# A fused threshold attention and gated MLP on one core: its 4602 steps in another order, and its PSUM banks handed out anew

## The chip, the core and the metric

The kernel runs on one core of a Trainium2 chip. The metric is device microseconds of one execution, from the first to the last instruction of that core with what lies around them. Its engines are TensorE (PE, with its weight loads as PEld), VectorE (DVE), ScalarE (ACT), GpSimd (POOL) and SyncE (SP), which here only issues transfers. Each runs its own list of instructions in order and waits for the others by semaphores. PSUM, where PE writes its results, has 8 banks.

## The reference

Attention with a threshold, over 8 batches and 8 heads (576 positions, 64 wide), feeds a gated MLP (512 in, 1024 inner, half of it a gate that mixes positions):

```python
scores = scale * np.matmul(q, k.transpose(0, 1, 3, 2))
thresh = np.max(scores, axis=-1, keepdims=True) - tau
scores = np.where(scores >= thresh, scores, -1000000000.0)
attn = np.exp(scores - np.max(scores, axis=-1, keepdims=True))
attn = attn / (np.sum(attn, axis=-1, keepdims=True) + 1e-09)
x = np.matmul(attn, v)                       # heads side by side: (8, 576, 512)
h = gelu_tanh(x @ w_in)
u, v = h[..., :512], h[..., 512:]
v_n = (v - mean(v)) / sqrt(var(v) + 1e-06) * g_ln
v_s = np.einsum('ts,bsd->btd', w_sg, v_n) + b_sg[None, :, None]
return x + (u * v_s) @ w_out
```

## The kernel before

Two heads are one attention, so there are 32 (n = 0 to 31), four to a batch, and behind each batch its MLP. The function doesn't compute where it is called: each step (a piece of work on one engine, or a transfer) goes into a list, `plan`, of 4602 steps. At the end `issue` runs through them in the order of a table of numbers, ORDER, that `table` unpacks; where an exponential follows a gelu or the other way round, it adds an ACT table load and a small activation on a spare column (L1156). The order in which the steps are issued is the order in which each engine's list stands. A second table, FIRST_BANKS, gives each PSUM tile its bank in the order of the steps; a step that writes a bank waits until the last reader of what lay there is done. So one table sets what stands behind what on every engine, the other who waits for whom at the banks.

The steps of an attention with n of 4 and more, with the names that the rows have:

- scores (L547): for a tile of 128 rows of one head, four matmuls of 288 columns (`ks`, `klz` with `qst`), six for the tile of both heads' last rows (`kl` with `qtail`). Nine tiles.
- DVE takes the negated maxima of the rows (L556, `maxima_of`); POOL makes the threshold of it (L562, with `columns`); ACT the exponentials (L583, into `p_0` to `p_3`, or `pm` for the tile of last rows); DVE keeps those over the threshold and sums each row (L590, "select"), after which the scores' bank is free.
- DVE turns blocks of 32 by 32 of the exponentials (L605, and L601 for `pm`) into `turned`.
- PE multiplies these with the values `v` (L743): 18 blocks, each with 8 small matmuls on tiles of 32 rows by 64 columns, in six steps of 24 (a row "x72" in an order below is three such steps; each matmul is recorded twice in the trace, so 144 there). ACT takes the result from PSUM (L750).
- The inverses of the row sums go from DVE (L628, L654) through DRAM and back (L658, L662: two transfers of SP's queue), and POOL multiplies with them (L754, `ir`). ACT and POOL split the result into two parts, `xh` and `xl` (L771, L776).

The MLP of a batch is made of products (L841) with weights split in two parts: v (512 columns, `wih`, `wil` with `xh`, `xl`), u, the spatial gate (`wsh`, `wsl` with `z`), down (`woh`, `wol` with `gh`, `gl`). Around them are gelu on ACT (L830), the normalisation (L920 to L957 on DVE, POOL and ACT), the fold of the last 64 rows on DVE (L901, `vt`), and the gate (L995 DVE, L1011 ACT, L1015 POOL). The first four attentions take another way (L527, and transpositions on PE, L252). The MLP of a batch lies in time beside the attentions of the next one, woven by ORDER.

Of the kernel before, what the change touches and what calls it, by code (L numbers as in the profile page):

```python
# [22 lines left out]
P = 128  # L23
# [10 lines left out]
    "c-m!H2V4|K-`=^q-Mixsj*cL`_a+ewsHjP7!4hMOCN}J`BpTamd83IX(bx;95H%W&5le_I5mbm3r1#zg1n!P<{g`iOW)FRT-|vo{otghU&+{)cy9Y%<_Jb~{"  # L34
    "g#h21{<taAE$Ki=M*2*vaF<;P$sh-Z*O5tli)Y|FGIjuxWt?#z=qE8zQhl73J~C*6#eaR=IMD!zuJ^#u0Dv3`766C=S%fW+9UdnG+)~Ki6Eif1r^pbR>*G;I"
    "v=Sh3Y=c=5Mjs>==mQBfQN%jRL(9<@c?}2_M3^`#fLqUEVk!#0*CNlbJEjN_WUL$^^|9D2KE%WnClZ;V0nP<3awJi>i^ZXNf`LN-`z7>o;e?n3`$Tc^GE-sk"
    "l(-k54lxp|#43F4rSLsOw?GV4EQ**?QS2W(qK18DYA!Bf6+$&b78FE_5x5AVQ87d-&=(n*u{ThKphOU=MHHTd2v0<@6bKXdAWI0b84JmdL2QZHMU<Kn^-^XO"
    ")nld>vFp@am5A6I7NNhQkt%issv%a(4vN$wH4A~JSa!CH;jve05i5rs6k{gVkRn%=X-<s@L@F^w@X&}z&FvR7X{vN?1H7LhcA7(g5DP#9tR!|4UDzScfP$<y"
    "7>t#|aU!n?H)3PESOqJB4IWv7u4o;FC1EwFp$H*1fOsu3qtrMx$a!{@!qXH7fM`%OkvTgKDQ<vlNz8?okWT-`=eDRR2BzA?eL@I{7!n;KlOi4?OG3ilQbadS"
    "CBi}FfhD6WB(71Mt3(^bqD45BIAwS_u|W6S0{lhf7#?@AcNBIKM-CrrsD&ajKs+HtBnB*jMySD|!hyrSv3bIi??OXy=Vbp;O8B_*lj5onBU6x6E9ONF2`Mxs"  # L40
    "kE{`L`60--V`AY9G`Jx?_Ma<Uw?Bg<okB_j`<3AEYf!OKXqd!_03k~*oe+C1#Cd%8Ai%`zGVYOpBgtYxicla8LJd;J{^14@p%L7t$c#|Um5>nEG26j3LgXep"
    "i{r~SIPiEKvcqr?O&|-h<20E49Xw71>QK1Feh^C3gPagf7ev~SDN@c+i8OctdykwFB5?G@@nRbd{?kCy^9>_IOlLZk$s8s$1%e{M;3Q&ZO}`RE-fvA|VsxP>"
    "(wO=<nnH@$Ag?Kc!tFa#v?=Tn$pS@i`ya<#R!s4MCIKjp5a)n&HIU5WOj4wQ1f19qD?CL&An}aE9GP(CL-<Wv;Ct^PBrGUgLd4EaYfXtFtXvhDWN1Vt;bfY@"
    "*~e?S;E@VMz?3OskaL6L0)wN6Qm<wDD^c@)SSaG?yIkRQY{Q_9VhSS~(Biyt2fmQ(03l}r$pDTQ-Ybv`AE^&CL-r0=Qkan}#TCp@ra_I6@S+B-fm%X`bZ96>"
    "Yl^1Oqyz_>OAQ9+YJ}=PqWTYO2H7%L2Dad4F{c)#11};-DA?#+;LZ?Xzc<7Q?yBV?#Bf-wLQ0FR7*m-t$Op{DurXvkU~#qmqOg$=jj<WR)0l+O;(12Ppr}J6"
# [71 lines left out]
Q = 32  # L117
# [1046 lines left out]
```

## Time and profile before

| | us |
|---|---|
| timed runs, median of 3 | 861.12 |
| lowest, highest | 858.95, 861.51 |
| profiled execution | 867.9 |
| its span, first to last instruction | 866.0 |
| mean granted clock of TensorE in it | 0.988 |

| engine | busy us | share of the span |
|---|---|---|
| PE | 829.8 | 96% |
| DVE | 679.7 | 78% |
| ACT | 602.0 | 70% |
| POOL | 583.4 | 67% |

Busy time is counted where an engine runs an instruction; waiting for a semaphore is idle time. What ended an idle time stands behind it as a releaser; "issue" is idle time in which the engine waited for nothing that the profile shows. The granted clock is 1.00 at full speed; 0.50 is the lower of two levels.

### The profile page before, as it was taken

How to read it: one execution, taken by the hardware profiler on the slowest of the kernel's cores; microseconds unless marked ns; L12 is line 12 of the kernel's file. 1: busy time of each engine (PE TensorE's matmuls, PEld its weight loads, DVE VectorE, ACT ScalarE, POOL GpSimd, SP SyncE). 2: the span in 40 equal slices, each digit the busy share in tenths (PEclk: the TensorE clock that was granted, in tenths of full speed). 3: DMA queues.
4: the chain of work that ended last, by engine and by line, in shares of the span. 5: the costliest groups of instructions: out<-in, count | busy, mean ns of one | idle time of the engine just before them, and what ended most of it. 6: DMA issues, size and time to landing. Idle time of an engine off the chain costs nothing.

```text
span 866.0 us, 30568 instructions
## 1 busy us (share of the span) xinstructions
PE 829.8 (96%) x12590; PEld 743.3 (86%) x12590; DVE 679.7 (78%) x1288; ACT 602.0 (70%) x1093; POOL 583.4 (67%) x966
## 2 busy tenths in 40 slices
PE   7999999988999999899999999999999999899998
PEld 5566789987889988899889988999899998799998
DVE  7898978976699888778887899789897988777110
ACT  5899987554976678666797468866688647774243
POOL 4885576573776667565867487856778567655486
PEclk8999999998999999999999999999999999999999
DMA  6645146554456565456555575465646656433101
GB/s 211 229 123 149 32 126 173 162 164 129 122 155 183 172 177 172 112 170 171 154 153 161 155 200 166 124 176 172 183 130 178 177 157 166 119 104 86 39 8 62
DMA packets 80190, 125.57 MB, mean 145 GB/s; under 512 B 13746, under 2 KB 36274, under 8 KB 80051
## 3 DMA queue, kind: packets, MB, share of 16 engines
q1 hardware_dynamic: 80050, 123.62, 49.4%
q8 instruction: 99, 1.62, 0.8%
q14 instruction: 41, 0.33, 0.1%
HBM read 70.55 MB, written 9.90 MB: 93 GB/s over the span
## 4 chain that ended last, share of the span: by engine, by line
PE 43%; DVE 4%; ACT 4%; issue 3%; POOL 2%; DMA 2%; SPq 1%; POOLq 0%; DVEq 0%; ACTq 0%
PE all_banks L841 28%; PE all_banks L547 8%; PE all_banks L743 7%; DVE maxima_of L556 2%; ACT p L583 1%; DVE p L590 1%; DMA ir<-ld 1%; ACT L1156 1%; DVE turned L605 1%; POOL free L1048 1%; POOL ot L1048 1%; SPq L662 0%; DMA rq<-in_qT 0%; SPq L470 0%; DMA ks<-khi 0%
## 5 line engine op out<-in xcount | busy, mean ns | idle before, releaser
L583 ACT ACTIVATE p<-all_banks,maxima_of 128x576 f32<-128x576 f32 x256 | 182.7, 738 | 95.3 <-DVE maxima_of L556 90.8
L556 DVE TENSOR_REDUCE maxima_of<-all_banks 128x1 f32<-128x576 f32 x288 | 206.8, 742 | 40.4 <-PE all_banks L547 33.0
L590 DVE SCALAR_TENSOR_TENSOR p<-all_banks,maxima_of,p 128x576 f32<-128x576 f32 x256 | 201.3, 806 | 42.3 <-ACT p L583 24.7
L547 PE MATMUL all_banks<-ks,qst 128*128 128x288 f32 x560 | 155.2, 310 | 7.9 <-DVE p L590 4.3
L605 DVE STREAM_TRANSPOSE turned<-p 128x1152 f32<-128x1152 f32 x112 | 152.4, 1367 | 7.2 <-PE all_banks L743 6.2
L743 PE MATMUL all_banks<-turned,v 32*64 32x144 f32 x8064 | 147.3, 286 | 11.1 <-issue 10.7
L743 PEld LDWEIGHTS all_banks<-turned,v 32*64 32x64 f32 x8064 | 127.6, 130 | 25.4 <-issue 22.8
L562 POOL TENSOR_TENSOR maxima_of<-columns,maxima_of 128x1 f32<-128x1 f32 x288 | 53.2, 191 | 115.7 <-DVE maxima_of L556 110.9
L547 PE MATMUL all_banks<-klz,qst 128*128 128x288 f32 x448 | 125.5, 298 | 0.0
L547 PEld LDWEIGHTS all_banks<-ks,qst 128*128 128x128 f32 x560 | 102.9, 190 | 22.2 <-DVE p L590 11.8
L841 PE MATMUL all_banks<-wsh,z 128*128 128x288 f32 (+2 forms) x512 | 111.7, 299 | 3.1 <-DVE pm L590 2.0
L1156 ACT ACT_TABLE_LOAD x81 | 103.9, 1283 | 1.5
L841 PEld LDWEIGHTS all_banks<-wsh,z 128*128 128x128 f32 x512 | 85.1, 190 | 4.7 <-DVE pm L590 2.2
L547 PEld LDWEIGHTS all_banks<-klz,qst 128*128 128x128 f32 x448 | 85.5, 191 | 1.8 <-issue 1.2
L841 PE MATMUL all_banks<-gh,woh 128*128 128x288 f32 (+2 forms) x256 | 75.8, 300 | 0.5 <-ACT ot L1045 0.5
L841 PE MATMUL all_banks<-gh,wol 128*128 128x288 f32 (+2 forms) x256 | 75.1, 296 | 0.0
L841 PE MATMUL all_banks<-wsl,z 128*128 128x288 f32 (+2 forms) x256 | 75.0, 297 | 0.0
L841 PE MATMUL all_banks<-xl,wih 128*128 128x288 f32 (+2 forms) x256 | 74.5, 296 | 0.0
L841 PE MATMUL all_banks<-xh,wil 128*128 128x288 f32 (+2 forms) x256 | 74.4, 295 | 0.0
L841 PE MATMUL all_banks<-xh,wih 128*128 128x288 f32 (+2 forms) x256 | 74.0, 296 | 0.0
L841 PE MATMUL all_banks<-gl,woh 128*128 128x288 f32 (+1 forms) x240 | 70.9, 299 | 2.5 <-POOL gl L1015 2.2
L1048 POOL TENSOR_TENSOR ot<-ot,xl 128x288 f32<-128x288 f32 (+1 forms) x60 | 47.8, 800 | 23.7 <-ACT ot L1045 23.4
(150 smaller groups left out, 1890.8 us busy)
## 6 DMA issues: line engine op xcount, KB each, us to landing
v<-in_vR SPq DMA_DIRECT2D x112, 288.0 KB, 3.5
ks<-khi SPq DMA_DIRECT2D x112, 144.0 KB, 3.2
rq<-in_qT SPq DMA_DIRECT2D x28, 320.0 KB, 4.3
qst<-qhi SPq DMA_DIRECT2D x56, 160.0 KB, 3.3
qst<-rq SPq DMA_DIRECT2D x56, 160.0 KB, 2.8
rk<-in_kT SPq DMA_DIRECT2D x28, 288.0 KB, 4.4
klz<-kl SPq DMA_DIRECT2D x56, 144.0 KB, 2.6
ir<-ld SPq DMA_DIRECT2D x56, 144.0 KB, 3.9
```

Source lines behind the costliest of these rows:

```text
L547: nc.tensor.matmul(sc[:, a, 0:HALF], w, x, start=(j == 0), stop=(j == len(terms) - 1))
L556: nc.vector.tensor_reduce(nmax, st["s", h, i][:, :, 0:HALF], AX.XY, ALU.max, negate=True)
L562: nc.gpsimd.tensor_tensor(thr, toff, st["nm", h, i], ALU.subtract)
L583: nc.scalar.activation(target(h, i), st["s", h, i][:, :, 0:HALF], AF.Exp, bias=st["nm", h, i])
L590: nc.vector.scalar_tensor_tensor(dst, st["s", h, i][:, :, 0:HALF], st["thr", h, i], dst, ALU.is_ge, ALU.mult, accum_out=st["l"][:, c:c + 1])
L605: nc.vector.transpose(out, st["p", i].rearrange("p (h k x) -> p k h x", h=2, x=Q))
L743: nc.tensor.matmul(st["accs"][g // 2][hs, g % 2, 0:W], st["v"][rows, o:o + D], st["turned"][rows, k, h * W:(h + 1) * W], start=(k == 0), s ...
L841: nc.tensor.matmul(st["acc"], *term(j), start=(j == 0), stop=(j == n - 1))
L1048: return lambda: nc.gpsimd.tensor_tensor(o(), o(), x[b, m][:, ts_], ALU.add)
L1156: tables[kind]()
```

## The change

Only the two tables change: ORDER, with the same 4602 steps in another order, and FIRST_BANKS. The code below them is the same, two lines further up in the file, so L743 is L741 after, L547 is L545, L841 L839, L754 L752, L562 L560, L605 L603, L590 L588. All matmuls are the same ones, 12590 in the trace. As exponentials and gelus stand in another sequence, `issue` adds two more table loads (84 switches for 82).

```diff
 ORDER = (
-    "c-m!H2V4|K-`=^q-Mixsj*cL`_a+ewsHjP7!4hMOCN}J`BpTamd83IX(bx;95H%W&5le_I5mbm3r1#zg1n!P<{g`iOW)FRT-|vo{otghU&+{)cy9Y%<_Jb~{"
...
 FIRST_BANKS = (
-    "c-l3R3lak{2txgP{~PyVw$o{5V-SJFw%nq|tut!JDkj6NSj{8HBD(-YS~c5BimM%nspK4jar(?HWA%AFD`a)pc1;UnP79di&}i?nWhlpK!+cAjNA+UD6oU;i"
...
```

What it moves is seen in the engines' lists. First PE in the values of attention 29, from the first of them on (before; in the trace this begins at 742.08 us):

```order
L743 MATMUL all_banks<-turned_11212,v_29_11287 64x144 x72
L547 MATMUL all_banks<-ks_1_11260,qst_138 128x288
L547 MATMUL all_banks<-klz_141,qst_138 128x288
...
L743 MATMUL all_banks<-turned_11212,v_29_11287 64x144 x48
L547 MATMUL all_banks<-ks_1_11260,qst_138 128x288
L547 MATMUL all_banks<-klz_141,qst_138 128x288
L547 MATMUL all_banks<-ks_1_11260,qst_138 128x288
L547 MATMUL all_banks<-klz_141,qst_138 128x288
L743 MATMUL all_banks<-turned_11212,v_29_11287 64x144 x24
L841 MATMUL all_banks<-wih_110,xh_9597 128x512
```

and the same place after:

```order
L741 MATMUL all_banks<-turned_11210,v_29_11297 64x144 x48
L545 MATMUL all_banks<-ks_1_11299,qst_138 128x288
L545 MATMUL all_banks<-klz_141,qst_138 128x288
...
L741 MATMUL all_banks<-turned_11210,v_29_11297 64x144 x72
L545 MATMUL all_banks<-ks_1_11299,qst_138 128x288
L545 MATMUL all_banks<-klz_141,qst_138 128x288
L545 MATMUL all_banks<-ks_1_11299,qst_138 128x288
L545 MATMUL all_banks<-klz_141,qst_138 128x288
L839 MATMUL all_banks<-wih_110,xh_9596 128x512
L839 MATMUL all_banks<-wil_114,xh_9596 128x512
L839 MATMUL all_banks<-wih_111,xh_10067 128x512
L839 MATMUL all_banks<-wil_115,xh_10067 128x512
L741 MATMUL all_banks<-turned_11210,v_29_11297 64x144 x24
```

The values come in pieces of 48, 72 and 24 where they came in 72, 48 and 24, with ten matmuls of the scores between the first two in both, and the last piece now stands behind four wide products. As many matmuls of PE lie ahead of the first row in both orders.

Then POOL, at the multiplication with the inverses of attention 13 (355 to 362 us), before:

```order
L562 TENSOR_TENSOR maxima_of<-columns,maxima_of 128x1
L927 TENSOR_SCALAR bn_4_5142<-bn_4_5142 64x1
L931 TENSOR_TENSOR bn_4_5142<-bn_4_5142,columns 64x1
L935 TENSOR_SCALAR bn_4_5142<-bn_4_5142 64x1
L754 TENSOR_TENSOR ir_5039<-v_13_4808,ir_5039 128x576
L562 TENSOR_TENSOR maxima_of<-columns,maxima_of 128x1 x3
L942 TENSOR_TENSOR vv_4_5115<-vv_4_5115,g_bc 64x512
L440 TENSOR_TENSOR kl<-rk_4887,khi_5144 128x576
```

and after:

```order
L929 TENSOR_TENSOR bn_4_5151<-bn_4_5151,columns 64x1
L560 TENSOR_TENSOR maxima_of<-columns,maxima_of 128x1
L933 TENSOR_SCALAR bn_4_5151<-bn_4_5151 64x1
L438 TENSOR_TENSOR kl<-rk_4890,khi_5144 128x576
L560 TENSOR_TENSOR maxima_of<-columns,maxima_of 128x1 x2
L940 TENSOR_TENSOR vv_4_5116<-vv_4_5116,g_bc 64x512
L752 TENSOR_TENSOR ir_5040<-v_13_4776,ir_5040 128x576
L955 TENSOR_TENSOR zt_101<-vv_4_5116,zt_101 64x512
```

The multiplication stood ahead of three thresholds and now stands behind them.

Last DVE in the scores of attention 9 (237 to 244 us), before:

```order
L605 STREAM_TRANSPOSE turned_3221<-p_0_2994 128x18x2x32
L556 TENSOR_REDUCE maxima_of<-all_banks 128x1 x3
L590 SCALAR_TENSOR_TENSOR pm,sums_of<-all_banks,maxima_of,pm 128x576
L605 STREAM_TRANSPOSE turned_3221<-p_1_3112 128x18x2x32
L901 TENSOR_TENSOR vt_3281<-all_banks,vt_3281 64x512
L590 SCALAR_TENSOR_TENSOR p_2_3272,sums_of<-all_banks,maxima_of,p_2_3272 128x576
```

and after:

```order
L603 STREAM_TRANSPOSE turned_3226<-p_0_3005 128x18x2x32
L554 TENSOR_REDUCE maxima_of<-all_banks 128x1 x3
L603 STREAM_TRANSPOSE turned_3226<-p_1_3147 128x18x2x32
L588 SCALAR_TENSOR_TENSOR p_2_3267,sums_of<-all_banks,maxima_of,p_2_3267 128x576
L899 TENSOR_TENSOR vt_3279<-all_banks,vt_3279 64x512
L588 SCALAR_TENSOR_TENSOR p_2_3267,sums_of<-all_banks,maxima_of,p_2_3267 128x576
L588 SCALAR_TENSOR_TENSOR pm,sums_of<-all_banks,maxima_of,pm 128x576
```

The select of pm, which came ahead of the second turn, is now the last of these. On PE the four matmuls of the next scores now take the bank that the first select of p_2 frees; in before they took the bank of pm.

## Rows read from the trace of the kernel before

**Rows 1.** Page, busy time: the span, and busy us (share) xinstructions of each engine

```profile
span 866.0 us, 30568 instructions
...
PE 829.8 (96%) x12590; PEld 743.3 (86%) x12590; DVE 679.7 (78%) x1288; ACT 602.0 (70%) x1093; POOL 583.4 (67%) x966
```

**Rows 2.** Lines: op, names, shapes xcount, busy us, mean ns, idle us before <-releasers

```profile
L547 PE MATMUL all_banks<-ks,qst 128*128 128x288 f32 x560 | 155.2, 310 | 7.9 <-DVE p L590 4.3 <-issue 2.6 <-ACT v L750 0.3
L743 PE MATMUL all_banks<-turned,v 32*64 32x144 f32 x8064 | 147.3, 286 | 11.1 <-issue 10.7 <-DVE uu L995 0.3
```

**Rows 3.** PE's time line: start, us, operation xcount, [idle before <-releaser]

```profile
196.18 2.50 PE L743 MATMUL all_banks<-turned,v 32*64 32x144 f32 x144 [2.08 <-issue]
...
205.38 0.78 PE L743 MATMUL all_banks<-turned,v 32*64 32x144 f32 x14 [2.83 <-issue]
...
330.08 0.54 PE L547 MATMUL all_banks<-ks,qst 128*128 128x288 f32 x2 [1.59 <-issue]
```

**Rows 4.** Page, DMA queues: packets, MB, share of 16 engines

```profile
q8 instruction: 99, 1.62, 0.8%
```

**Rows 5.** Windows: us, then busy us (xcount) of PE, PEld, DVE, ACT, POOL, PEclk, DMA, GB/s

```profile
235.86:330.07 94.21, 90.25 (x1655) 82.23 (x1655) 84.72 (x156) 67.91 (x117) 66.39 (x108) 1.00 0.59 169
```

**Rows 6.** PE's time line, attention 29

```profile
742.08 2.51 PE L743 MATMUL all_banks<-turned,v 32*64 32x144 f32 x144
...
745.91 0.29 PE L547 MATMUL all_banks<-ks,qst 128*128 128x288 f32 x1 [0.65 <-issue]
...
747.05 1.78 PE L743 MATMUL all_banks<-turned,v 32*64 32x144 f32 x96
...
752.12 0.74 PE L743 MATMUL all_banks<-turned,v 32*64 32x144 f32 x28 [1.80 <-issue]
...
753.12 0.39 PE L841 MATMUL all_banks<-wil,xh 128*128 128x512 f32 x1
753.35 0.40 PE L841 MATMUL all_banks<-wih,xh 128*128 128x512 f32 x1
```

**Rows 7.** Windows, the stretches of lower granted clock (eighth column, PEclk)

```profile
200.00:220.00 20.00, 17.16 (x209) 14.82 (x208) 12.75 (x24) 10.95 (x18) 7.73 (x16) 0.83 0.46 129
320.00:340.00 20.00, 18.40 (x319) 16.84 (x306) 13.67 (x24) 15.90 (x28) 15.04 (x22) 0.91 0.53 149
360.00:380.00 20.00, 18.64 (x307) 18.12 (x311) 14.84 (x27) 11.60 (x21) 12.98 (x21) 0.91 0.52 150
```

**Rows 8.** PE's time line, three idle times put down to DVE and POOL

```profile
361.36 0.40 PE L841 MATMUL all_banks<-wsh,z 128*128 128x288 f32 x1 [1.97 <-DVE pm L590]
...
438.40 0.40 PE L547 MATMUL all_banks<-ks,qst 128*128 128x288 f32 x1 [1.35 <-DVE p L590]
...
610.41 0.40 PE L841 MATMUL all_banks<-gl,woh 128*128 128x288 f32 x1 [1.25 <-POOL gl L1015]
```

**Rows 9.** POOL's time line, attention 13

```profile
358.89 1.40 POOL L754 TENSOR_TENSOR ir<-v,ir 128x576 f32<-128x576 f32 x1 [2.59 <-ACT vv L939]
360.25 0.47 POOL L562 TENSOR_TENSOR maxima_of<-columns,maxima_of 128x1 f32<-128x1 f32 x3
```

**Rows 10.** DVE's time line, attention 9

```profile
236.99 1.38 DVE L605 STREAM_TRANSPOSE turned<-p 128x1152 f32<-128x1152 f32 x1 [0.79 <-PE all_banks L743]
238.30 2.05 DVE L556 TENSOR_REDUCE maxima_of<-all_banks 128x1 f32<-128x576 f32 x3
240.27 0.80 DVE L590 SCALAR_TENSOR_TENSOR pm<-all_banks,maxima_of,pm 128x576 f32<-128x576 f32 x1
...
242.29 0.64 DVE L901 TENSOR_TENSOR vt<-all_banks,vt 64x512 f32<-64x512 f32 x1
```

**Rows 11.** PE's time line, attention 9: the idle time in the same stretch

```profile
242.99 0.40 PE L841 MATMUL all_banks<-wsh,z 128*128 128x288 f32 x1 [0.59 <-DVE vt L901]
```

**Rows 12.** Page, the costliest groups: the table loads of ACT

```profile
L1156 ACT ACT_TABLE_LOAD x81 | 103.9, 1283 | 1.5
```

**Rows 13.** PE's time line, the start

```profile
13.52 0.69 PE L252 MATMUL all_banks<-ident_r,p 128*128 128x128 f32 x2 [2.14 <-DVE p L590]
```

More of the change, by code (lines that the diff above doesn't have):

```diff
@@ L38 @@
[L38 to L45, printed above, removed]
@@ L98 @@
[L98 to L100 removed]
+    "c-n1P30zcF)PLtOZ{7?u0}QC3?4Tfvptxq>hUS)Nrj=SQh?-k!i&k1$xm0SYNv^n?TDj$txuX~=iVGm1Ae#%a4lv9<bHBU10l)9}Ilk@QbN=Ul{`cJb?t|kv"
+    "gz$mS_=@l7Jv$+(i#ES<hnN}bc5nzB^iDdl9_iF_0qg}d1VT>VSNoiB5)lVbD@3sYw>mh9nq=*S2IOpP;lT1h4tRwLamOtVMw}v2H-}{Bzz7bolR&(k1E&U<"
@@ new lines @@
+    "2ku4=9<c`!0XGpp+(B?0G%?&tFdgh5PAn2>CnO0j(9pz$V2}=AoG6NvCN{v`gbO9e039St5|Mat&dezw<&9W7foP?SfMIY{O^LqqmP$wsrLjc>TMEiaS(0vt"
+    "B(SqAh$qdRQl}uu;Y#blfE$$t{GSdMI9xe{61x~kEG1{ap7hMoj%GT(&S6%PcBCMUN+XS<q*)r32B(jKQ*fM7K_L;oa*AeG8WnrsE@Ys13etdYh%K=sHq8<}"
+    "a#HG520PDj3M2WklA#e5%+1J($k~O@N~xrA9AqSBxB>SPVn*Vrz^zDWRN$QGk2qp%!V!ZhX?lb<BE3ioOQN;P${tbcM5BN$CM2eT01|a+IE>ty047164cG;d"
+    "c9I3<N$8T`l%s<2p}{#~hG-)TM?GowB%E|B%~IA#V@e14F%YZ->7lvOq%k+jKvI%4v_48b&iX~@e?PMp24rlJh9rtuh8$6qBQZGzb0ZO*D$?q}4Fro^NH;?z"
@@ new lines @@
+    "j)<mD`;9Ck!e07kWPw_+6p~cVIv{6h!6QyIDm4@(5pcW7nGI5~VKlNE7MAj(Wy&EV3*pp*7A+Z6&Z%$fLMtu6A`_ROaV={n2_%)1g2_(wW9hYw7WU*sHad*A"
+    "b6{J3m^kMwS!bFpwJFj8WfM;t1gTIIMv>-CVj`2%g-XKF+)W%UJ`S0Pp=feeyAxY9kv4odE1sxDftW2tGSNqBBy#vF8mX~}m?f<|d=X9Lz!o%R91_zsA(0Yc"
+    "Ff1B<pg81A(HUPHp0<)qh%2SYd|KB%7RM<J&6xJ%W<=Q$EQ~;IC~=HQvuE(ckEP<A>NI_ZN!ukUa0^An=oH#S!6iD3qbQ{$wsbHz$^<b7DND)=nOdz0M?!|O"
+    "Lo}E(U94)$0JP-FB#;J68aSFFiHaeJ80?Xq7&&rKEs#X6l`M&GVgpLb1KS}fK}mP!&(NIJ!kJp?g5^pXG2z5lVzrz(gctx*L8==ZQqqD(rYTc)92H$O<2E@b"
@@ new lines @@
+    "S+hhr=YUcUoRcbzKq`@=s<o(xCxqy1<D7LWN>Ny%xLa;!?Br$|iK9X|GowQ(XVDlEAtvd}G%!*5*j#0jJ7<ze8{}rWBoCb{5)-L}NH9V{5}Uxv8Im+il%{Bw"
+    "(*kdi{gvIE(~e~>Z6HN6_sXV@Dup;ne6fY8iHR&#xO44i<s(&_S(+bm`an`=?c^DmiDb^#hTM#pnsl}i(U4ivl=u@*IaPx#5x9@Thp9znM14iGh-1p>LLiNf"
+    "+$@qvaubbelBOp0mO^r722a_sGfvmcri&bzS)pQ3Gt-T5AW?7+BE!Qm7c8<_&axtR<bmi;`{^D{GGxiq_zaU6(dd*3O^nhaaY?I$Dkr|oiZYV3ZtBG`DqO2>"
+    "1X{4rjM$rzBG9BcDM`YeFr;Ha9Fdt}P${LmmTv`irS7dC6%5h&pAcgw%2&dmVQ4fu8dN{IS)xy(QvIDDEmTo6_sZ7=V$e)Fvjo91k%CYKne0vr8WG7YtSp#B"
@@ new lines @@
+    "EknhGk~nclpad98ITf7^1d_^*4U#h=$AS@TDKUn^wWjIBqJvMQmlBuinaxlODFZrAh-5Ff2=u~)VY-{8$wSJ+LM$wDR#c>V1Wu|JX$TOqFqYI=aHiNYMu?6z"
+    "$4NuNNeLh}U7X@L#bpzNl_}29f&}Wx-XM~UsP$VC$<5sV^TEkd!CXmlE!#uF4zUVGEwxK429KYBENs-V4=G=KA+RJjoS?v2h<+Bfp%=_8+Z&QFjgOs(A9f<%"
+    "IAaSjqmM*D+(|)512Lvc7D2`jBthC|p)@5X0)`L>3LP-w)RHG{C)nhkhNjZDC?!~&TOy98LBdjQ1ewIfA;^RC<C&$5&xkQZ)R5Yfpo~1Wk&r1-PSVIi+$iz?"
+    ")9TcRdeb`sNBt=n>5$?{xziAoBx6m%7>qO`l&;0843(V<&17T@sR>m|ut<>+6N?(qCaNnbTzW6nlZ3-e2{T5G`V&IV4K>MEvXZu8&TSWgK#Z8cbfHnGGeWPH"
@@ new lines @@
+    "Xv=fUBlpT59-O=L*1v8zSHo9ZT0iw#uhKV=^TU&CL2vywZ2jBHD{MHf_0Ke~PA~3%1#G3|{N3Qe(HkGPe?8yaeDl5D3nuXivp2%BM!8L}xao&qP$paz>IJ0`"
+    "na4+E@`)L7kmra>m-FtX_&fF}g+-^*d+Jh*m-wuxim+@MA6yVsp?CAHjMNpkF*d^7|BRLGgU)w_CxOqt*ru+q+6@k+%;4cb!q}|(mqu-HzZ2T>AXI_u!F=h2"
+    "!?rLRYUpv<A@g%@w&{lFIn;OjUE~F!R`-}QK60D9IB4)COWeJ%(qd&K^3I1u^#RMk6Wv`3M;s19<sChq)c35f6D{7Zjb{08lY*XV+tgYu?W!HfO{KF&JcW8c"
+    "ZINHGFAiDeX>-jP{KQ)ACsP^fQ0%k1isq@+_J1`Q^F(cd`!h|KLS={hLHGK}YtO3M^(q!ZFLY}N5JC@y+^t;xElfGvzgp&UdHkCNcX@Z-f9uN`zNLExbkZN1"
@@ L108 @@
+    "b@6c!4T+-oo7+?ApZ=qC?<a4Hl<7%ZxIC&X<f!|Xf9(<<9I##anE=18)|+-B{01;GPh)sgZ^stwI|WTuYisSfJ;h<;k$i{z<@6r#-=OmyjGE;IsoE>zm9Wia"
+    "VeA0?o@FEZ9z^~CrO*i3"
 )
```

106 lines of the change are left out of this document (45 added, 61 removed).

## The prediction

> **What bounds the kernel now.** I read the page's busy shares first, then what ended PE's idle time, then the time line around each stall, then the granted clock of those stretches. PE is busy 96% of the span, DVE 78%, ACT 70%, POOL 67% [rows 1]: the kernel is PE's list of 12590 matmuls plus the holes in it. The same matmuls are issued after the change, so only holes and clock can move.
>
> The holes are of three kinds.
>
> *Holes that no engine explains.* "Issue" ends 10.7 us of the idle time before L743 and 2.6 us of that before L547 [rows 2], 13.3 together. One hole of 2.08 us stands at the first matmul of a value step (the run that follows it has no cut behind it on the grid below) [rows 3]; I take it for a wait on data and leave it out: 11.2 us. The rest stand inside runs of matmuls. Queue q8 carries instructions: 99 packets of 1.62 MB, 16.4 KB each [rows 4], so 12590/99 = 127.2 matmuls with their weight loads to a packet. From the stall at 235.87 to the one at 330.08 PE runs 1655 matmuls [rows 3, 5], 13 times 127.3. In the values of attention 29 the count can be done by hand: between the stalls at 745.91 and 752.12 stand 8 matmuls of L547, 96 of L743, 4 of L547 and 20 of L743 (the run is one of 48, and 28 come behind the stall) [rows 6], together 128. So these are places where PE has used up a packet and the next has not landed. Why there: 144 matmuls of L743 take 2.51 us, 17 ns each [rows 6], and the 127 before 745.91 are nearly all of these, some 2.4 us of work; the 8 of L547 between 745.91 and 747.05 take some 0.13 us each, one of 512 columns 0.23 us [rows 6]. A packet of such matmuls lasts 15 us or more (127 times 0.13 is 16.5) and hides the fetch; one of L743 alone does not.
>
> *Clock.* The granted clock over 200 to 220 us is 0.83, over 320 to 340 us 0.91, over 360 to 380 us 0.91 [rows 7], where most of the span has 1.00: 20 us times the missing share is 3.4, 1.8 and 1.8 us. In each, PE had sat idle just before: 2.83 and 1.59 us for fetches [rows 3], 1.97 us for DVE [rows 8]. In the stretch PE went to the lower of its two levels, 1.2 GHz. Idles of 2.08 and 1.80 us [rows 3, 6] drew no fall, so a long idle is not always enough.
>
> *One wait on POOL, seen as waits for DVE and for POOL.* The hole of 1.97 us before 361.36 is put down to DVE's select of pm [rows 8]. Behind it: POOL's multiplication by the inverses (L754) starts only at 358.89, after 2.59 us idle, and the three thresholds (L562) queued behind it come at 360.25 [rows 9]; DVE's select needs one. L754's inverses come back through DRAM in two transfers. The holes of 1.35 us at 438.40 and 1.25 us at 610.41 [rows 8] have the same head of queue, as has one of 0.97 us at 412.75: four, 5.5 us.
>
> **The change, part by part.** The sum is made against the profiled execution, 867.9 us (span 866.0 [rows 1], 1.9 around it). That is 6.8 us above the 861.12 median of the runs shown; I come back to that.
>
> 1. *Fetches.* From the order I count, packet by packet, the matmuls from the point where a fetch can start to the one that needs it; with the stalls above as marks that is some 142 (a packet and about 15), and its work by the spacings of [rows 6] is the cover. In before five such stretches hold at most 3 matmuls that are not of L743, with 2.4 to 2.8 us of cover, and three pairs of poor stretches follow each other within 5.8 us of work. After has no stretch with under 7, and its worst pair has 6.3 us. At attention 29 the first value piece shrinks from 144 recorded matmuls to 96, the 144 come second, the last 48 move between wide products: the two stretches that lasted 2.4 and 3.6 us hold about 3.3 and 3.5 us. Bounds: all 11.2 us go (-11.2), or only the stalls of the five thinnest, 3.4 us in all, two of them in [rows 3, 6] (-3.4). The first pair, near 205 us, gets only 0.4 us of cover against a stall of 2.83 us [rows 3], and some stretches have 3.4 us of cover as in before, where one in ten stalled by 0.3. I leave 2.7 us: **-8.5**.
>
> The Trainium skill ("Runtime: NRT & Kernel Launch", section "Instruction fetch mechanics") says that each engine refills 16 KiB blocks of 256 instructions and that crossing a block is mostly hidden, because dispatch is slower than the refill. The size agrees with the 16.4 KB packets; that it is hidden does not agree with holes on a grid of 127 matmuls. By that rule this term, and the clock term that follows, would be zero.
>
> 2. *Clock behind fetch stalls.* -3.4 and -1.8 if the holes of 2.83 and 1.59 us shrink [rows 3, 7]; I charge 1.9 for the chance that what remains near 205 us, or a new wait, still draws one: **-3.3** (0 to -5.2).
>
> 3. *POOL's wait.* At attention 13 the order puts L754 behind the three thresholds and the gain, so its DMA has the time in which they run; the 1.97 us and the 1.8 us of low clock go. At attention 16 one threshold still follows it directly, but its consumer stands 3.5 us of PE work further on than before (13.3 against 9.8), so the 1.35 us go. (Such a distance is counted in the order: PE's work, at the spacings above, from the last product that the inverses need to the first matmul that needs the threshold.) At 15 the distance falls from 12.6 to 11.9, at 23 it is 10.2 in both: those stay, the first grows by 0.7; a new one at 26 (11.6 us, where 11.1 and 12.6 stalled and two of 12.1 to 12.7 did not) I price at 0.4. -1.97 - 1.8 - 1.35 + 0.7 + 0.4 = **-4.0** (bounds -5.1 to +1.5: the upper one has 15 and 26 stall by 2 us each and keeps one fall of the clock).
>
> 4. *DVE at attention 9.* In before the select of pm follows three maxima, frees a bank, and PE fills wide products meanwhile. In after the second turn (L605) and the select of p_2 come first, pm last, and PE's next four scores wait for p_2. DVE from the end of the values: 1.3 (turn), 2.0 (three maxima), 1.3 (turn), 0.7 (select) = 5.3 us [rows 10]. PE has 14 matmuls of L547 (1.9) and 8 wide ones (1.8) = 3.7 us: a hole of 1.6. Then vt and the next select, 0.6 + 0.7, against four scores, 0.5: 0.8 more. In before vt cost 0.59 us there [rows 11]. 2.4 - 0.6 = **+1.8** (0 if DVE runs ahead; +5.2 with a fall of the clock such as the first of [rows 7]).
>
> 5. *Two more table loads.* One is 1283 ns [rows 12] with a small activation behind it, some 1.5 us; two are 3.0 us of ACT, which is busy 70% [rows 1] and is seldom named as what PE waits for. **0** (0 to +3.0).
>
> 6. *Start.* The first exponentials are followed by a transposition that PE waits 2.14 us for [rows 13]; the order now has the cast of a spatial weight on ACT ahead of them, loads that weight earlier, and issues the first exponentials in another order. **-0.5** (-1.5 to +2.8, if that cast waits for its load).
>
> 7. *The other waits of DVE, each under 0.7 us.* Both orders have about as many places where a bank is freed late: **0** (-2 to +2.5).
>
> Sum: -8.5 - 3.3 - 4.0 + 1.8 - 0.5 = **-14.5**, 853.4 on the profiled execution. The timed runs are 6.8 us shorter; if that difference lies in stalls that the change removes, they gain 7.7 and end at 853.4; if none of it does, they gain all and end at 846.6. Fetches meet other transfers, which differ from run to run, so I think that most of it lies there: **853**, own range 846 to 858.
>
> **Rivals.**
>
> *A. The change doesn't do what it says:* the holes have a cause that the count of matmuls doesn't place, and the new order keeps them. For it: the first pair near 205 us stalled 2.83 us and an equally poor one elsewhere hardly at all. Against it: the grid of 127. Then only points 3, 4 and 6 are left, -2.7: 858.4. The rule cited above (the Trainium skill, "Runtime: NRT & Kernel Launch", section "Instruction fetch mechanics") would lead to this time as well.
>
> *B. DVE takes the freed time.* It is busy 78% of the span [rows 1], and each score's bank comes free only with its select. If PE comes 14 us earlier to selects that are no earlier, the holes come back as waits for DVE. Against it: 22% of DVE's span is free. 861, give or take 2.6.
>
> *C. Slower: the holes at attention 9.* 1.6 and 0.8 us of idle within 3 us, more idle than the 1.59 that was followed by a fall of the clock [rows 3, 7]. Price 1.8 + 3.4 = 5.2, and all selects behind are that much later. It decides once the fetch stalls give back less than that, as they would if the same amount of stalls moved to the stretches of 3.3 to 3.6 us, of which after has some twenty. Then 861.1 + 5.2 - 2.0 (half of point 3) = 864.
>
> **How the numbers follow.** 0.3% is 2.6 us, about what a measurement here can tell from no change. Forecast 0.64 (all of it faster), A 0.13 (half faster, half the same), B 0.12 (0.08 the same, 0.02 each way), C 0.11 (slower). Faster 0.64 + 0.065 + 0.02 = 0.73 (rounded up), the same 0.14, slower 0.13. The range takes the forecast's low end, 846, and goes up to 862 to hold A and most of B.
>
> **What the profile of the changed kernel would show.** Right: "issue" before L743 and L547 under 5 us in all; no stall inside the values of attention 29; granted clock 1.00 near 330 and 370 us; no hole at attention 13; one of 1 to 2 us near 240 us that ends with a select. Wrong: holes by "issue" still 8 us or more in all, on a grid of 127 matmuls at other places (point 1 fails), or DVE waits of PE up by as much as the fetch stalls fell (B).

## The result, and the profile after

The changed kernel takes 845.62 us (median of 6 runs, 843.32 to 853.52) against 860.19 of the kernel before in the same comparison (858.86 to 861.95): 14.6 us less, ratio 0.9845 with a 95% interval of 0.980 to 0.989. Later, on another occasion, it was 846.2 against 862.2, ratio 0.983 (0.9803 to 0.9857). The forecast was 853, with 846 to 862 as its range: the median is 0.4 us under it. The sum of the terms was -14.5; I had spent half of it on the difference between the profiled execution and the timed runs. Further down, four runs of two kernels that were over 1.5% above their fastest are left out of the medians.

The profiled execution of the changed kernel took 849.7 us. Its page begins:

```profile
span 847.9 us, 30583 instructions
...
PE 823.4 (97%) x12590; PEld 739.8 (87%) x12590; DVE 679.0 (80%) x1288; ACT 603.8 (71%) x1097; POOL 584.8 (69%) x966
```

The span is 18.1 us shorter than in [rows 1]. PE does the same 12590 matmuls in 6.4 us less of busy time, and the rest is idle time. The 6.4 us are hardly the change's: in a second execution with PE's order of before (the run of POOL's step below) PE is busy for 823.5 us, as here. Most of that is the clock of the execution that I had read. The groups of matmuls that answer to [rows 2] (same columns):

```profile
L545 PE MATMUL all_banks<-ks,qst 128*128 128x288 f32 x560 | 154.4, 309 | 8.3 <-DVE p L588 3.6 <-DVE pm L588 3.6 <-issue 0.5
...
L741 PE MATMUL all_banks<-turned,v 32*64 32x144 f32 x8064 | 146.2, 286 | 6.6 <-issue 4.8 <-DVE turned L603 1.4 <-DVE uu L993 0.3
```

Idle time by issue is 5.3 us where it was 11.2; under 5 was forecast. The waits for the select of pm have come instead (3.6). PE's time line in the values of attention 29, which answers to [rows 6]:

```profile
726.46 1.78 PE L741 MATMUL all_banks<-turned,v 32*64 32x144 f32 x96
729.04 0.40 PE L545 MATMUL all_banks<-ks,qst 128*128 128x288 f32 x1 [0.81 <-DVE p L588]
...
730.76 2.51 PE L741 MATMUL all_banks<-turned,v 32*64 32x144 f32 x144
...
734.86 1.04 PE L741 MATMUL all_banks<-turned,v 32*64 32x144 f32 x48
```

In this execution no run is cut: the stalls of 0.65 and 1.80 us are gone. (In the second profile of this kernel, below, the last piece is cut, for 0.70 us.) In their place stands one wait of 0.81 us for a select, since the piece ahead of it is now 0.8 us shorter. Two of the seven fetch stalls that are left, the longest:

```profile
153.35 1.93 PE L741 MATMUL all_banks<-turned,v 32*64 32x144 f32 x100 [1.51 <-issue]
...
199.88 0.37 PE L741 MATMUL all_banks<-turned,v 32*64 32x144 f32 x7 [1.02 <-issue]
```

At attention 9 the new hole came as worked out (DVE, then PE):

```profile
231.31 1.36 DVE L603 STREAM_TRANSPOSE turned<-p 128x1152 f32<-128x1152 f32 x1
232.82 0.82 DVE L588 SCALAR_TENSOR_TENSOR p<-all_banks,maxima_of,p 128x576 f32<-128x576 f32 x1
```

```profile
233.70 0.40 PE L545 MATMUL all_banks<-ks,qst 128*128 128x288 f32 x1 [1.80 <-DVE p L588]
...
235.08 0.40 PE L545 MATMUL all_banks<-ks,qst 128*128 128x288 f32 x1 [0.59 <-DVE p L588]
```

1.80 and 0.59 us; 1.6 and 0.8 were forecast. The granted clock by stretches, to be read against [rows 7] (PEclk is the eighth column):

```profile
200.00:220.00 20.00, 20.00 (x126) 17.70 (x126) 16.34 (x29) 17.74 (x28) 13.89 (x23) 1.00 0.54 156
220.00:240.00 20.00, 17.26 (x356) 15.35 (x355) 16.48 (x33) 17.07 (x30) 14.34 (x24) 0.91 0.59 149
300.00:320.00 20.00, 19.94 (x289) 17.66 (x293) 15.12 (x30) 14.44 (x24) 15.37 (x27) 0.91 0.61 168
```

The low level is gone behind the fetch stalls and has come behind attention 9 and at 300 us. There, and at 402 us, are two holes of the kind of [rows 8]:

```profile
300.06 0.40 PE L545 MATMUL all_banks<-ks,qst 128*128 128x288 f32 x1 [1.99 <-DVE pm L588]
...
402.38 0.40 PE L545 MATMUL all_banks<-ks,qst 128*128 128x288 f32 x1 [1.58 <-DVE pm L588]
```

The first is at attention 11, which I had passed over; the second, at 15, was forecast (0.97 + 0.7). Attention 13 has none; its multiplication comes last on POOL, where [rows 9] had it first:

```profile
349.41 0.33 POOL L560 TENSOR_TENSOR maxima_of<-columns,maxima_of 128x1 f32<-128x1 f32 x2
350.18 1.29 POOL L940 TENSOR_TENSOR vv<-vv,g_bc 64x512 f32<-64x512 f32 x1 [0.43 <-ACT vv L937]
351.44 1.43 POOL L752 TENSOR_TENSOR ir<-v,ir 128x576 f32<-128x576 f32 x1
```

PE's idle time of one profiled execution each, sorted by what it waited for, is thus (us; "start" is all that lies before 100 us):

| | before | after |
|---|---|---|
| start | 6.9 | 5.1 |
| fetches ("issue" within runs) | 11.2 | 5.3 |
| the turn of pm at attention 7 (2.08 in [rows 3]) | 2.1 | 1.4 |
| other waits for DVE, POOL, ACT | 10.6 | 7.7 |
| sum | 30.8 | 19.5 |
| span less sum | 835.2 | 828.4 |

### The profile page after: what moved, and what is told of

Read it like the earlier page. It is cut to its first block, busy times and chain, and to the rows that moved or that the text cites. A ratio compares the mean times of both kernels' runs of the same rounds, so it can differ in the third digit from the quotient of the medians.

```text
span 847.9 us, 30583 instructions
## 1 busy us (share of the span) xinstructions
PE 823.4 (97%) x12590; PEld 739.8 (87%) x12590; DVE 679.0 (80%) x1288; ACT 603.8 (71%) x1097; POOL 584.8 (69%) x966
## 4 chain that ended last, share of the span: by engine, by line
PE 70%; DVE 7%; DMA 6%; ACT 6%; POOL 4%; issue 4%; SPq 2%; POOLq 0%; DVEq 0%; ACTq 0%
PE all_banks L839 40%; PE all_banks L545 13%; PE all_banks L741 13%; DVE p L588 3%; ACT L1154 2%; ACT p L581 1%; DMA qst<-qhi 1%; DVE turned L603 1%; DVE maxima_of L554 1%; PE all_banks L727 1%; DMA ir<-ld 1%; PE all_banks L525 1%; PE all_banks L250 1%; DMA ks<-khi 1%; DMA w<-in_w_in 1%
## 5 line engine op out<-in xcount | busy, mean ns | idle before, releaser
L588 DVE SCALAR_TENSOR_TENSOR p<-all_banks,maxima_of,p 128x576 f32<-128x576 f32 x256 | 201.7, 806 | 35.6 <-ACT p L581 20.7
L545 PE MATMUL all_banks<-ks,qst 128*128 128x288 f32 x560 | 154.4, 309 | 8.3 <-DVE p L588 3.6
L603 DVE STREAM_TRANSPOSE turned<-p 128x1152 f32<-128x1152 f32 x112 | 152.0, 1364 | 12.0 <-PE all_banks L741 10.8
L741 PE MATMUL all_banks<-turned,v 32*64 32x144 f32 x8064 | 146.2, 286 | 6.6 <-issue 4.8
L741 PEld LDWEIGHTS all_banks<-turned,v 32*64 32x64 f32 x8064 | 127.3, 130 | 20.2 <-issue 15.6
L545 PE MATMUL all_banks<-klz,qst 128*128 128x288 f32 x448 | 124.3, 296 | 0.0
L545 PEld LDWEIGHTS all_banks<-ks,qst 128*128 128x128 f32 x560 | 101.8, 188 | 23.3 <-DVE p L588 10.2
L560 POOL TENSOR_TENSOR maxima_of<-columns,maxima_of 128x1 f32<-128x1 f32 x288 | 53.5, 193 | 86.7 <-DVE maxima_of L554 79.5
L839 PE MATMUL all_banks<-wsh,z 128*128 128x288 f32 (+2 forms) x512 | 112.8, 299 | 0.0
L839 PEld LDWEIGHTS all_banks<-wsh,z 128*128 128x128 f32 x512 | 85.9, 191 | 1.4 <-issue 1.0
L545 PEld LDWEIGHTS all_banks<-klz,qst 128*128 128x128 f32 x448 | 84.6, 189 | 0.5
L839 PE MATMUL all_banks<-gh,wol 128*128 128x288 f32 (+2 forms) x256 | 75.2, 297 | 0.0
L839 PE MATMUL all_banks<-gh,woh 128*128 128x288 f32 (+2 forms) x256 | 75.1, 296 | 0.1
L839 PE MATMUL all_banks<-wsl,z 128*128 128x288 f32 (+2 forms) x256 | 75.1, 298 | 0.0
L839 PE MATMUL all_banks<-xl,wih 128*128 128x288 f32 (+2 forms) x256 | 74.5, 295 | 0.0
L839 PE MATMUL all_banks<-xh,wih 128*128 128x288 f32 (+2 forms) x256 | 74.2, 295 | 0.0
L839 PE MATMUL all_banks<-xh,wil 128*128 128x288 f32 (+2 forms) x256 | 73.8, 295 | 0.0
L839 PE MATMUL all_banks<-gl,woh 128*128 128x288 f32 (+1 forms) x240 | 70.2, 295 | 0.3 <-POOL gl L1013 0.3
L839 PE MATMUL all_banks<-wih,xh 128*128 128x512 f32 x160 | 63.5, 400 | 0.0
```

The lines of the kernel that those rows point to most:

```text
L545: nc.tensor.matmul(sc[:, a, 0:HALF], w, x, start=(j == 0), stop=(j == len(terms) - 1))
L560: nc.gpsimd.tensor_tensor(thr, toff, st["nm", h, i], ALU.subtract)
L588: nc.vector.scalar_tensor_tensor(dst, st["s", h, i][:, :, 0:HALF], st["thr", h, i], dst, ALU.is_ge, ALU.mult, accum_out=st["l"][:, c:c + 1])
L603: nc.vector.transpose(out, st["p", i].rearrange("p (h k x) -> p k h x", h=2, x=Q))
L741: nc.tensor.matmul(st["accs"][g // 2][hs, g % 2, 0:W], st["v"][rows, o:o + D], st["turned"][rows, k, h * W:(h + 1) * W], start=(k == 0), s ...
L839: nc.tensor.matmul(st["acc"], *term(j), start=(j == 0), stop=(j == n - 1))
```

## The experiments

My theory was the sum: fetch stalls placed by the count of PE's instructions, the clock behind them, POOL's head of queue, and one loss at attention 9. The rivals: the stalls have a cause that the count doesn't place, or the holes are of the kind that, taken away at one place, come back at the next.

**Moving the packets, not the order.** The changed kernel's order stands untouched. Behind the last warm-up matmul at the start stand n small ones, each two weight loads and two matmuls of 16 columns:

```diff
-            nc.tensor.matmul(x[:, 0:2 * P], pm[:, 0:P], pm[:, 0:2 * P], start=True, stop=True)
+            w = 2 * P if k < 3 else 64
+            nc.tensor.matmul(x[:, 0:w], pm[:, 0:P], pm[:, 0:w], start=True, stop=True)
+            for j in range(18 if k == 3 else 0):
+                rows, out = slice(j % 4 * Q, j % 4 * Q + Q), slice(j // 4 % 2 * D, j // 4 % 2 * D + D)
+                nc.tensor.matmul(all_banks[out, j % 4, 0:16], pm[rows, 0:D], pm[rows, 0:16], start=True, stop=True)
```

With n = 18, 72 instructions:

> The changed kernel, its order untouched, with 18 small matmuls (72 PE instructions) put behind the warm-up matmuls at the very start, which are made narrower by about what the small ones take. Every instruction packet of PE then ends 72 instructions earlier in the work. If the fetch stalls are placed by the count of PE instructions: counted as for the prediction, 11 stretches would have under 3 us of cover and 9 pairs stand too close (changed kernel: 0 and 2; kernel before: 5 and 6, with 11.2 us of stalls), so the idle time by issue rises from 5.3 to 18 to 26 us, a few of the stalls lower the granted clock, and the time rises from 845.6 to 860 to 875. Rival (stalls are placed by time, by other transfers, or by what stands beside them, and the order removed them in another way): issue stays at 4 to 8 us and the time at 844 to 850.

It took 876.9 us (872.9 to 882.5; ratio to the kernel before 1.019, 1.012 to 1.026). Idle time by issue was 26.4 us in all. The group of the values:

```profile
L745 PE MATMUL all_banks<-turned,v 32*64 32x144 f32 x8064 | 151.8, 288 | 24.8 <-issue 23.3 <-DVE turned L607 1.4
```

The windows run from one stall to another (PE's count is in brackets behind its busy time):

```profile
302.36:331.90 29.54, 28.18 (x382) 25.09 (x381) 21.24 (x38) 20.47 (x34) 20.92 (x35) 0.89 0.50 137
331.90:351.68 19.78, 18.50 (x254) 16.60 (x255) 18.18 (x33) 17.92 (x31) 14.32 (x23) 1.00 0.50 145
408.33:431.46 23.13, 21.12 (x382) 18.88 (x382) 20.49 (x38) 16.91 (x28) 17.19 (x29) 1.00 0.56 164
634.96:685.37 50.41, 49.11 (x763) 45.93 (x764) 40.47 (x75) 37.09 (x66) 39.32 (x59) 0.97 0.56 157
```

382, 254, 382 and 763 matmuls are 3, 2, 3 and 6 packets of 127.2. Nothing in the order of any engine was changed, and 31 us came: the rival is out, and the expectation was on the low side.

With n = 64, 256 instructions, a whole packet (here two warm-up matmuls are narrow):

> The changed kernel with 64 small matmuls (256 PE instructions, one whole packet) at the same place, two warm-up matmuls made narrow for them. The packets cut the work where they do in the changed kernel. If the count places the stalls, issue is 4 to 8 us and the time that of the changed kernel plus up to 3 us for the longer start: 845 to 850. If adding small matmuls at the start does something by itself (clock, a queue, a shift in time of everything behind), it moves as the run with 72 does, or by more.

848.4 us (847.1 to 851.4), and issue 3.8 us in all:

```profile
L745 PE MATMUL all_banks<-turned,v 32*64 32x144 f32 x8064 | 146.1, 286 | 4.1 <-issue 3.1 <-DVE turned L607 0.7 <-DVE uu L997 0.2
```

Many more small matmuls, and no harm beyond the longer start: it is where the packets cut, not that something was added. With n = 48, 192 instructions:

> The changed kernel with 48 small matmuls (192 PE instructions) at the start, two warm-up matmuls made narrow for them. Counted as before, 5 stretches then have under 3 us of cover and 3 pairs stand too close, nearly what the kernel before has (5 and 6), while everything else is the changed kernel's. If the time depends on this count: 8 to 12 us idle by issue, and 849 to 857 us: the difference to the changed kernel and to the run with 256, which has the same longer start (848.4), is what the placing of the fetches is worth in the change (by the profiles 4 to 6 of the 14.6 us). If fetches are the whole gain: 858 or more. If only very bad placings matter: 846 to 849, as with 256.

867.6 us (ratio 1.006, 1.003 to 1.010), issue 19.2 us:

```profile
L745 PE MATMUL all_banks<-turned,v 32*64 32x144 f32 x8064 | 151.9, 287 | 20.0 <-issue 17.4 <-DVE turned L607 1.4 <-DMA v<-in_vR 1.0
```

This expectation missed: 7 us of stalls and 11 us of time lie above its ranges. A threshold at 3 us of cover is too sharp, and it doesn't say how long a stall is. Counted over all twelve traces of this document, at the spacings of [rows 6], stretches (a packet and 15 matmuls) of under 3 us stalled by 0.2 us or more in 31 of 42 cases, of 3 to 4 us in 71 of 269, of 4 to 6 us in 25 of 239, and longer ones in none of 626; here 17 places did. But the time followed the stalls: from n = 64 to 48, 19.2 us for 15.4 us of stalls, to 18, 28.5 for 22.6, that is 1.25 and 1.26 us each (the clock falls behind some of them). These factors are rough. The run with 48 was timed on another occasion, where the kernel before took 862.1 us and not 860.2; with that taken off it is 1.12. By the spans of the profiled executions it is 1.23 and 1.46.

That the stalls are waits for packets can be read from the traces directly, since they record each packet of q8. In the twelve traces there are 127 stalls of 0.2 us or more by issue, leaving out the wait of 2.08 us of [rows 3]. Every one ends 1.2 to 1.7 us after such a packet has landed, and 2.2 to 3.3 us after its transfer began. All 127 stand within 3 matmuls of one grid with a step of 127.3, the same for both orders and every shift. The wait of 2.08 us has its last packet 11.8 us ahead: it was right to leave it out.

The kernel before, shifted by 80 instructions:

> The kernel before with 20 small matmuls (80 PE instructions) at the start, one warm-up matmul made narrow for them. Counted as before, 9 stretches have under 3 us of cover and 9 pairs stand too close, about what the changed kernel with 72 has (11 and 9), which took 876.9 us with 26.4 us idle by issue. If the count decides for either order: 20 to 28 us idle by issue and 872 to 885 us; with equal stalls its distance to 876.9 is what the change brought beside the fetches (by the profiles 8 to 10 us, so 882 to 888). Rival (the order before is less sensitive, its stalls have another cause): 858 to 866.

870.2 us (ratio 1.010, 1.006 to 1.014), issue 15.8 us without the wait of 2.08: the stalls rose as they do with the other order, by less than I said, and the time came out below the range. At 15.8 us of stalls the changed order would take 848.4 + 1.26 * 12.0 = 863.5 on the line of its own runs; the order before takes 7 us more, or 5 with the 1.9 us between the two occasions taken off. So, as an estimate, a third to a half of the 14.6 us is left for all that isn't fetches. It rests on one profile each, and this one has 3.6 us of waits of PE for transfers of data, where no other has over 1.0.

**POOL's head of queue alone.** In the kernel before, one step is moved (1408 is the multiplication of attention 13, 1453 the last of the three thresholds):

```diff
+    order.remove(1408)
+    order.insert(order.index(1453) + 1, 1408)
```

> The kernel before with one step moved: POOL's multiplication with the inverses of attention 13 (L754) is issued behind the three thresholds that stood behind it; PE's order and the banks are untouched. If that head of queue made the 1.97 us hole at 361 us, and the hole the fall of the clock behind it: no hole of over 0.5 us there, granted clock 1.00 over 360 to 380, and 3.8 us less (856 to 858). Rival (DVE or the DMA is late by itself, and POOL's order only shows it): the hole stays within 0.5 us of 1.97 and the time at 859 to 862. Second rival: the hole goes and the clock falls anyway: 2 us less.

860.52 us against 860.22, ratio 1.000 (0.997 to 1.003): nothing. In its profile the hole is gone, as is the wait on POOL, but 0.90 us stand a few matmuls on, for POOL's zt, which was queued behind (PE):

```profile
358.60 0.81 PE L841 MATMUL all_banks<-wt,zt 128*128 128x288 f32 x4 [0.90 <-POOL zt L957]
```

That the hole is gone doesn't show that the move took it away. In the profile of the next run (the start alone), where POOL's order is that of before, the multiplication and the thresholds behind it come at once (POOL):

```profile
349.90 1.43 POOL L754 TENSOR_TENSOR ir<-v,ir 128x576 f32<-128x576 f32 x1 [0.36 <-issue]
351.29 0.49 POOL L562 TENSOR_TENSOR maxima_of<-columns,maxima_of 128x1 f32<-128x1 f32 x3
```

PE has no hole over 0.3 us there, and neither has it in the kernel before shifted by 80. The transfers of the inverses took 1.4 us and up to 3.8 us from issue to landing in that run, 2.9 and up to 5.0 in the execution of [rows 9]. So the hole differs from one execution to the next, as these transfers do, and the run with the step moved doesn't tell what the place of the multiplication is worth.

And the clock: the run with POOL's step moved has PE's order of before, and a fetch stall as long as the 1.59 us of [rows 3] (PE):

```profile
326.15 0.53 PE L547 MATMUL all_banks<-ks,qst 128*128 128x288 f32 x2 [1.67 <-issue]
```

Yet the windows that answer to [rows 7] read

```profile
320.00:340.00 20.00, 18.29 (x247) 16.80 (x247) 17.00 (x29) 17.54 (x31) 16.73 (x27) 1.00 0.65 190
360.00:380.00 20.00, 19.94 (x398) 18.98 (x397) 15.28 (x29) 12.81 (x25) 11.42 (x18) 1.00 0.53 158
```

where 0.91 stood twice. The stall at 205 us, 2.83 there, was 1.30 here and 0.54 in the next run. So the clock's falls inside the kernel, and much of that stall, belonged to the one execution that I read: its mean clock was 0.988, that of 49 other timed runs of the kernel before 0.990 to 0.998.

**The start alone.** In the kernel before DVE's second select of p_0 (217) is put ahead of the first of p_1 (226):

```diff
+    order.remove(217)
+    order.insert(order.index(226), 217)
```

> The kernel before with one step moved: DVE selects the second half of p_0 ahead of the first half of p_1, as in the changed kernel; ACT, PE and POOL as before. PE's first nine transpositions need both halves of p_0. If this order made the second hole at the start: 2.14 us shrink to 1.2 or less, and the low clock behind it, over 0 to 20 us, may rise from 0.83 towards the 0.91 of the changed kernel: 1 to 3 us less (857 to 860). Rival (the cast on ACT and the order of the exponentials made the difference, not DVE): the hole stays at 1.8 us or more, the time within 1 us of before.

857.88 us against 860.22, ratio 0.998 (0.994 to 1.001): 2.3 us, which the interval doesn't part from zero. The hole of [rows 13] became two small ones:

```profile
11.79 1.12 PE L252 MATMUL all_banks<-ident_r,p 128*128 128x128 f32 x4 [0.40 <-DVE p L590]
13.20 2.18 PE L252 MATMUL all_banks<-ident_r,p 128*128 128x128 f32 x9 [0.29 <-DVE p L590]
```

The clock of that stretch stayed as low as before:

```profile
0.00:20.00 20.00, 15.69 (x69) 10.36 (x71) 14.86 (x35) 11.23 (x20) 8.48 (x22) 0.83 0.66 228
```

(In the profile of POOL's step, whose start is that of before, the hole is 2.59 us and this clock 0.91.) So the order on DVE made most of the hole, and I had priced it at 0.5 us. In the changed kernel 0.5 us are left of it in both profiles; with the moves below, which don't touch the start, 0.5 to 1.4.

**Mending the changed kernel's three holes.** Each run moves steps of the changed kernel only; the last is all three moves:

```diff
+    order.remove(1030)
+    order.insert(order.index(1040) + 1, 1030)
+    order.remove(1240)
+    order.insert(order.index(1296) + 1, 1240)
+    order.remove(1576)
+    order.insert(order.index(1632) + 1, 1576)
```

The first two lines, DVE's second turn at attention 9:

> The changed kernel with one step moved: at attention 9 DVE's second turn (L603, 1.36 us) is issued behind the two selects of p_2 instead of ahead of them. If the order on DVE makes the hole there (1.80 us, then 0.59): the first shrinks to 0.3 to 0.6, the second stays; no low clock behind it; 1.3 to 3.2 us less than the changed kernel (842 to 844 if that is at 845.6). Rival (the exponentials or the thresholds end last there, and DVE waits for them in either order): a hole of 1.4 us or more stays and the time within 1 us of the changed kernel.

847.1 us. The hole shrank from 1.80 to 1.24 us only (with DVE's order as it was, four profiles, one of them shifted by the whole packet, have 1.5 to 1.8), and the clock fell behind it again, 0.91 over 220 to 240 us. DVE now waits for ACT, whose exponential of p_2 stands behind two other activations (ACT, then DVE):

```profile
232.71 0.74 ACT L581 ACTIVATE p<-all_banks,maxima_of 128x576 f32<-128x576 f32 x1
```

```profile
233.55 0.82 DVE L588 SCALAR_TENSOR_TENSOR p<-all_banks,maxima_of,p 128x576 f32<-128x576 f32 x1 [0.88 <-ACT p L581]
```

The other four lines, POOL at attentions 11 and 15:

> The changed kernel with two steps moved: POOL's multiplications with the inverses of attentions 11 and 15 (L752) are issued behind the thresholds that stood behind them. If these heads of queue make the holes at 300 us (1.99) and 402 us (1.58): both under 0.6, and 2 to 4 us less than the changed kernel (842 to 844). Rival, as the same move at attention 13 of the kernel before had it: the holes go and come back within 5 us as a wait for what now stands behind the multiplication or is queued late (there 0.90 us on POOL's zt), and the time stays within 1.5 us of the changed kernel.

847.0 us. At attention 11 the hole is gone. At 15 1.07 us stay, and another head of queue shows: ACT's copy of the next keys (L434) waits for a transfer to have read the buffer, and the exponential of pm stands behind it:

```profile
397.57 0.69 ACT L434 ACTIVATE khi<-rk 128x576 fp32r<-128x576 f32 x1 [2.85 <-DMA qst<-qhi]
398.16 0.72 ACT L581 ACTIVATE pm<-all_banks,maxima_of 128x576 f32<-128x576 f32 x1
```

All three moves:

> The changed kernel with the three moves of the two runs beside it together. If their gains add up: 3 to 6 us less than the changed kernel, about 840 to 842, and faster than both kernels. If the time they free is taken by other waits: within 2 us of the changed kernel.

847.4 us; at attention 15 1.53 us stay. And the changed kernel as it is, beside them:

> The changed kernel as it is, on the same chip as the three beside it and to be compared with them: 843 to 849 us. Its fetch stalls should fall on the same places as in its first profile (153.4, 199.9, 365.6, 493.1, 519.0, 710.8 us), as the count of PE instructions is the same, but differ in length: 4 to 7 us in all.

846.2 us (844.6 to 849.5). In this profile the hole at 300 us wasn't there at all, without any move, that at 402 us was 1.45, and issue 4.1 us in all; the stalls of 153 and 493 us had nearly gone (0 and 0.25). Three stalls, of 0.49, 0.61 and 0.70 us, stand where the first profile had none, on the same grid; I had expected the same places. None of the mended versions beats it: their medians lie within 1.2 us of each other, and their runs overlap. Holes that hang on a transfer differ from one execution to the next by as much as these moves are worth.

## Why the prediction was right, point by point

The direction and the mechanism of the largest term were right; most of the other terms were not. That the sum, -14.5, comes out at the measured 14.6 is luck: it was made against one execution with a low clock, held 5.1 us for falls of the clock that only that execution had, and twice what fetches turned out to be worth, and it left out other gains, at the start and in small waits.

1. *Fetches (-8.5).* The cause is shown: the count of PE's instructions places the stalls, each of them ends behind the landing of a packet, and moving the packets by 72 instructions costs 31 us with every engine's order unchanged. The size was too large by about half. In the profiled pair 11.2 fell to 5.3 us, -5.9. But three profiles of PE's order before have 11.2, 9.1 and 6.0, and five of the order after, with the mended kernels, 5.3, 4.1, 5.4, 6.8 and 5.7 (with the whole packet 3.8). With 1.1 to 1.5 us for each, the difference of the means (8.8 and 5.5) is worth some 4 us.
2. *Clock behind fetch stalls (-3.3).* This step failed, though the falls were gone as forecast. It took two falls of one execution for a property of the kernel; two more profiles of the same PE order have none, one of them with a stall of the same length (1.67 us). The fall behind POOL's wait in point 3 was of that execution too.
3. *POOL's wait (-4.0).* This step failed in its price: it took the wait of one execution for a property of POOL's order. The head of queue is there in every execution, but at attention 13 it cost 1.97 us in one profile and nothing in two others with the same POOL order, where the transfers came sooner. Moved alone, it was worth 0.0 us (within 2.6); in the changed kernel a hole of the same kind stood at attention 11 in one profile and not in the other. I had counted only waits whose consumer I found at once, and there the first threshold behind the multiplication had none on my list. Of the 5.5 us four such holes before, 3.9 us were left in the first profile after, and 1.5 in the second; but the same places hold 2.9 and 2.7 us in the other two profiles of PE's order before, and 0.3 in the shifted one. What the change does to them stays open.
4. *DVE at attention 9 (+1.8).* Right: 1.80 and 0.59 us, less the 0.59 of before; 1.76 and 0.59 in the second profile. That it is exact is partly luck: 1.6 and 0.8 were worked out.
5. *Table loads (0).* No idle time of PE is put down to them; no run took them away.
6. *Start (-0.5).* Probably too small: 1.7 us of holes in the profiled pair, 2.3 us when done alone, though that is not clear of zero.
7. *Other waits of DVE (0).* Too small as well: leaving the holes of points 3 and 4 out, they fell from 4.5 to 1.5 us (7.3 to 2.7 in the pair of the next paragraph), and the wait for the turn of pm at attention 7 from 2.1 to 1.4.

What remains open: fetches 4, start 2, points 3, 4 and 7 together 3 to 4, the turn of pm 0.7 make some 10 to 11 of the 14.6 us. Some 2 us may be clock (0.994 in the mean of the 49 timed runs of before, 0.9965 in 12 of after); no run parts it. Two executions that stand near the medians can be set side by side, POOL's step (860.2 us) and the second profile of the changed kernel (845.2 us): of the 14.9 us between their spans, fetches are 5.0, the start 2.2, the turn of pm 0.7, other waits 4.3, and 2.7 PE's busy time and the smallest gaps. So the fetches are some third of the gain, and only for them did runs that moved nothing else show a price clear of the noise. The rest is read from profiles.

The step that put the number at 853 and not at 846 was the last one, that the 6.8 us by which the profiled execution stood over the median lay in stalls that the change removes. Most of it was the clock of that execution, and it was no part of the gain. The rivals: A is out by the shifted packets and by the landings. B (waits for DVE take the freed time) did not happen; they fell too. C's hole at attention 9 was there, with the fall of the clock in one profile and without it in the other, and it decided nothing, as the stalls had not moved elsewhere.

On the rule of the Trainium skill ("Runtime: NRT & Kernel Launch", section "Instruction fetch mechanics") that crossing a block is mostly hidden: here 26.4 us of a span of 880.7 were waits for packets of instructions in one order of the blocks, and 3.8 of 847.6 in another. It agrees with the trace for stretches of a packet that hold over 6 us of PE's work, of which none stalled, and not for those of small matmuls.

## What to carry to other kernels

Where one engine issues many short instructions in a row, count them: its instructions come in packets of fixed size, and a packet that is run through in a few us isn't always hidden (here three in four stalled under 3 us, one in four at 3 to 4 us, none above 6 us). Spread such runs between long instructions, and try a few dozen idle instructions at the start, since a shift of the packets alone moved this kernel between 846 and 877 us; none of the shifts tried here made it faster. Read at least two executions before giving a price to a fall of the clock or a wait on a transfer: those of one trace may not be there in the next. And a wait at the head of a queue has the next one behind it; taking one away alone is often worth nothing.

## What the runs showed of the hardware

An instruction packet of 16.4 KB held 127 pairs of weight load and matmul. In 127 stalls PE went on 2.2 to 3.3 us after the transfer of its packet had begun and 1.2 to 1.7 us after it had landed; the stalls were 0.2 to 3.2 us long, different from run to run. I had not expected that falls of the granted clock follow idle times so loosely: 1.59 us drew one and 1.67 us at the same place of another execution did not; 2.39 us at attention 9, in two holes, drew one in one profile of the same kernel and none in the next; a fetch stall of 2.69 us in the kernel before shifted by 80 drew none.
